# Clustered attention and two mixtures: tile sizes in one pool, and a new order of stack copies, centroids and dots

## The chip, the cores and the metric

The kernel runs on one core of a Trainium2 chip, as one program. The metric is device microseconds for one execution, from the first to the last instruction with what lies around it; smaller is better. The profiler names the engines PE (TensorE, matmuls and transposes), PEld (TensorE's weight loads), DVE (VectorE), ACT (ScalarE), POOL (GpSimd) and SP (SyncE, which issues nearly all DMAs here).

## The reference

Attention with B=2, H=8, S=768, D=64 comes first; each query and key is given to the nearest of 16 centroids of its head, and a query sees the keys of its own cluster only. The result, as 1536 rows of 512, goes through two layers of the form (g(x @ w_in)) @ w_out, with 2048 columns between.

```python
q_n, k_n, c_n = (a / (norm(a) + 1e-6) for a in (q, k, centroids))
q_assign = argmax(einsum('bhsd,hcd->bhsc', q_n, c_n), -1)      # k_assign alike
mask = q_assign[:, :, :, None] == k_assign[:, :, None, :]
scores = where(mask, q @ k.T / sqrt(D), -1e9)
attn = softmax(scores) @ v                                     # then [1536, 512]
h = x @ w1_in;  x = (h * cos(h)) @ w1_out
h = x @ w2_in;  g = where(h >= 1, h, where(h <= -1, 0, (h + 1)**2 / 4));  out = g @ w2_out
```

## The kernel before

**Order.** The program sets each engine's order itself: an engine runs its instructions as the Python code writes them (`manual_schedule`). What stands first in a queue and waits holds up all that is behind it; this goes for SP's queue of DMA issues too.

**Attention.** There are 8 pairs (batch, two heads) and 16 cycles d = 0 to 15; a cycle is one head of a pair, 12 row tiles of scores. A cycle's order is a string of words, run by `run_cycle`: `S` scores of a row tile (4 matmuls, then DVE's row maximum), `E` its exponential on ACT, `T` and `t` a transposed tile of probabilities (copied out of PSUM by ACT or by DVE), `V` the product with v, `R` the inverse row sums (DVE, then POOL writes `line`, then SP stores it to DRAM as `flat`), `B` SP reads `flat` back, spread over 64 partitions, as `rb`, `X` DVE multiplies V's result by `rb`, `Y` POOL splits that into `xh` and `xl`, `W` and `w` a step of the weights' conversion, `P` the next step of preparing a pair, `K` the copies for a pair's second head. Even cycles run EVEN, odd ones ODD; the first is BEGIN, the last three have strings of their own.

**A pair's preparation** (`prep_pair`) has 12 steps. Steps 1 to 4 transpose q and k (`ptq`, L492), copy them out as `t32` (L498) and split them on POOL into `th` (L474) and `tl` (L475). Steps 5 and 6 are the dots with the centroids: matmuls `dt` (L513), ACT's copy `dc` (L516), transposes `pd` (L520). Steps 7 to 11 find the nearest centroid on DVE and POOL (`eq`, L532, is POOL's; the maximum after it, L537, and `dots`, L539, are DVE's); step 9 also issues `stack_head(0)`, four copies by SP (L470) from `th` and `tl` into the stacked operands `st0` and `st1` of the first head. Step 12 transposes the result to `oht` and copies it into the stacks, `one_hots(0)`, four small copies. For the second head, `stack_head(1)` and `one_hots(1)` together are one entry of the list `second`, which `K` runs. `th` and `tl` are one buffer each; pairs 1, 3 and 5 use the memory of a weight tile instead, so only pair 7 must wait until the copies out of pair 6's `th` and `tl` are done.

**The first pair** (`first_pair`) is prepared ahead of the cycles. `centroid_setup` normalises the centroids by a chain of small DVE steps (L265 to L275) after ACT's square root (L260). After the root, ACT runs an Exp (L262) whose result nobody reads: it loads ACT's table, and it writes two elements of `nat1`, so that the load of the second pair's q and k, into the same tile, has to wait for it. Its input is `y`, the column that L265 then overwrites.

**The mixtures.** A unit is `hidden` (h = x w_in for 512 columns and 512 rows) or `output` (y = g w_out): 48 matmuls of 512 columns in 4 groups, three per product, since x, w and g are each a high and a low fp32r part. A layer has 12 units of each kind, and hidden and output take turns. `hidden` multiplies the weights with `xh` and `xl`; `output` multiplies them with `gh` and `gl`. Four weight tiles go round: slices qi = 0 and 2 use `w_0` (hidden) and `w_1` (output), qi = 1 and 3 use `w_2` and `w_3`.

**Memory.** Tiles lie in a partition one behind the other, by pools. Ahead of `xpool` stand `xh`, `xl`, `w_0`, `w_1` and the weights' loading tiles, all at multiples of 512 bytes. `xpool` holds, in bytes per partition, `rec` 128, `den` 3 x 128, `turned` 128, `line` 512 and `rb` 2 x 1536: 4224, which is 8 x 512 + 128. What is allocated behind it, attention's tiles and, after attention, the mixtures' (`w_2`, `w_3`, `gh`, `gl`, the sums and scratch), follows from there: the mixtures' tiles all start 128 bytes behind a multiple of 512.

Of the kernel before, what the change touches and what calls it, by code (L numbers as in the profile page):

```python
# [9 lines left out]
F32 = mybir.dt.float32  # L10
# [4 lines left out]
AF = mybir.ActivationFunctionType  # L15
# [4 lines left out]
P = 128  # L20
# [13 lines left out]
def attention_moe_moe(  # L34
# [19 lines left out]
    B, H, S, D = q.shape  # L54
# [22 lines left out]
    desc = cpool.tile([P, C], F32, name="desc")  # L77
# [56 lines left out]
    xpool = ctx.enter_context(tc.tile_pool(name="xpool", bufs=1))  # L134
# [70 lines left out]
    with ExitStack() as actx:  # L205
# [48 lines left out]
        def centroid_setup(ct):  # L254
            sq = ct[:, 1]
            nc.vector.tensor_tensor(sq, ct[:, 0], ct[:, 0], ALU.mult)
            ss = ap.tile([P, 32], F32, tag="css", name="css")
            nc.vector.tensor_reduce(ss[:, 0:1], sq, AX.X, ALU.add)
            y = ss[:, 1:2]
            sq = nc.scalar.activation(y, ss[:, 0:1], AF.Sqrt)  # L260
            nat[1] = [w0pool.tile([P, 2, NJ, 2, D], F32, tag="wraw", bufs=1, name="nat1")]
            nc.scalar.activation(nat[1][0][:, :, 0, 0, 0:1].rearrange("p s o -> p (s o)"),  # L262
                                 y.to_broadcast([P, 2]), AF.Exp, scale=0.0)
            for _ in range(2):
                nc.vector.tensor_scalar(y, y, 1e-30, None, ALU.max)  # L265
                nc.vector.reciprocal(ss[:, 2:3], y)
                nc.vector.scalar_tensor_tensor(
                    ss[:, 3:4], ss[:, 0:1], ss[:, 2:3], y, ALU.mult, ALU.add)
                nc.vector.tensor_scalar(y, ss[:, 3:4], 0.5, None, ALU.mult)
            nc.vector.tensor_scalar(ss[:, 2:3], y, 1e-6, None, ALU.add)  # L270
            nc.vector.reciprocal(ss[:, 3:4], ss[:, 2:3])
            cd = ap.tile([P, HS], F32, tag="pt", bufs=PT_BUFS, name="cd")[:, :P].rearrange(
                "p (r d) -> p r d", r=2)
            for r in range(2):
                done = nc.vector.tensor_scalar(cd[:, r], ct[:, 0], ss[:, 3:4], None, ALU.mult)  # L275
            return cd, done

        prepped = {}
        second = []

        def first_pair():
# [28 lines left out]
            def bank(name):  # L310
                return pool_q.tile([P, HS], F32, tag="q", name=name)
# [5 lines left out]
            def turn(s, hf):  # L317
                qk[s, hf] = bank(f"qk0_{s}_{hf}")
                for jj in range(HJ):
                    nc.tensor.transpose(qk[s, hf][:, jj * P:(jj + 1) * P],  # L320
                                        t[:, s, hf * HJ + jj].rearrange("p h d -> p (h d)"), ident)
# [7 lines left out]
            pc = ps_t.tile([P, HS], F32, tag="t", name="pc")[:, :P]  # L329
            turn(0, 0)  # L330
            turn(0, 1)
            nc.tensor.transpose(pc, cd.rearrange("p r d -> p (r d)"), ident)
            turn(1, 0)
            turn(1, 1)
            run_idle(NIDLE[1])
            pcv = pc.rearrange("p (g h c) -> p g h c", h=2, c=C)
# [3 lines left out]
            for s, hf in ((0, 0), (0, 1), (1, 0)):  # L340
                nc.scalar.activation(t32[s][hf], qk[s, hf], AF.Copy,
                                     scale=D ** -0.5 if s == 0 else 1.0)
# [109 lines left out]
        def prep_pair(i):  # L452
# [4 lines left out]
            if i in (1, 3, 5):  # L457
                t2 = w0pool.tile([P, 2, 2, S], F32R, tag="w_1", name=f"t2_{i}")
# [10 lines left out]
            def copy(dst, src):  # L469
                nc.sync.dma_start(dst.bitcast(F32), src.bitcast(F32))  # L470
# [6 lines left out]
            def stack_head(h):  # L477
                rows = slice(h * D, (h + 1) * D)
                t = st[h][0]
                copy(t[0:D], th[rows, 0].unsqueeze(1).to_broadcast([D, 2, S]))  # L480
                copy(t[D:P, 0], tl[rows, 0])
                t = st[h][1]
                copy(t[0:D, 0], th[rows, 1])
                copy(t[D:P, 0], th[rows, 1])
                copy(t[0:D, 1], tl[rows, 1])
# [65 lines left out]
            def one_hots(h):  # L551
                for s in range(2):
                    for par in range(2):
                        r0 = par * 64 + s * 32 + h * C
                        dst = st[h][s][D:D + C, 1].rearrange(
                            "c (par jp n) -> c par jp n", par=2, n=P)[:, par]
                        copy(dst, oht[r0:r0 + C])

            def second_head():
                stack_head(1)  # L560
                one_hots(1)

            one_hots(0)
            second.append(second_head)
            yield

        units = [(i, h, hf) for i in range(len(pairs)) for h in range(2) for hf in range(2)]
# [24 lines left out]
        def row_exp(n):  # L592
            s, nm = ptile[n]
            d, jj = divmod(n, NJ)
            if jj == 0:
                dens[d] = xpool.tile([P, 32], F32, tag="den", bufs=3, name=f"den{d}")
            p = ap.tile([P, 2, HS], F32, tag="p", bufs=P_BUFS, name=f"p{n}")
            nc.scalar.activation(p, s[:, :, :HS], AF.Exp, bias=nm,  # L598
                                 accum_out=dens[d][:, jj:jj + 1])
            ptile[n] = p  # L600
# [23 lines left out]
        dens = {}  # L624
# [47 lines left out]


        NDBL = len(units) // 2
        rec = xpool.tile([P, 32], F32, tag="rec", name="rec")
        nc.gpsimd.memset(rec, 0.0)
        made = chain.from_iterable(prep_pair(i) for i in range(1, len(pairs)))

# [2 lines left out]
        def scores_of(n):  # L681
            scores(n, 0)
            scores(n, 1)
            row_max(n)

        def run_cycle(d, order):


            for word in order.split():
                what, arg = word[0], int(word[1:] or 0)  # L690
                n = NJ * d + arg
                if what == "S":
                    if n < NJ * NDBL:
                        scores_of(n)
                elif what == "E":
                    if n < NJ * NDBL:
                        row_exp(n)
                elif what in "Tt":
                    p_transpose(2 * d + arg // NJ, arg % NJ, what == "t")
                    next_slot()  # L700
                elif what == "P":
                    next(made, None)
                elif what == "R":
                    inverse(d)
                elif what == "V":
                    p_v(d)
                elif what == "X":
                    if opsum:
                        x_rows(min(opsum))
                elif what == "K":  # L710
                    if second:
                        second.pop(0)()
                elif what == "B":
                    spread()
                elif what == "Y":
                    if x32s:
                        x_parts()
                elif what in "Ww":
                    pump(1 if d >= FIRST + (what == "w") else 0)
                elif what == "N":  # L720
                    next_slot()
            if d == 3:
                issue_chunk(0)

        PRE = "P S8 P E8"
        BEGIN = "S3 P T0 T1 S4 E3 P T2 E4 P T3 S5 E5 t4 T5 S6 T6 T7 E6 P R S7 t8 T9 E7 T10 P S8 P E8 B P S9 P t11 S10 V E9 E10"
        EVEN = "P S5 T0 T1 P t2 E5 S6 T3 P T4 E6 t5 S7 R T6 P T7 E7 S8 X T8 T9 E8 Y t10 B S9 P w P E9 t11 S10 W E10 V"
        ODD = "K S5 T0 T1 P t2 S6 E5 T3 X T4 t5 S7 Y E6 P T6 R E7 T7 S8 P E8 t8 T9 S9 T10 B P t11 E9 W S10 V P P E10 W"
        LATE_ODD = "S5 T0 T1 t2 E5 S6 T3 K R T4 t5 S7 X Y E6 T6 T7 E7 S8 E8 t8 T9 S9 T10 B t11 S10 E9 V W W W E10"
        LATE_EVEN = "S5 T0 t1 t2 E5 S6 T3 T4 E6 R T5 S7 X Y E7 T6 S8 T7 t8 W S9 E8 t9 B T10 E9 t11 W S10 V E10 W"  # L730
        LAST = "S5 T0 E5 t1 T2 T3 X t4 R t5 Y t6 T7 t8 B T9 t10 T11 W V W W W X Y"
        first_pair()
        for d in range(-1, NDBL):
            run_cycle(d, PRE if d < 0 else BEGIN if d == 0 else
                      {13: LATE_ODD, 14: LATE_EVEN, 15: LAST}.get(d, (EVEN, ODD)[d % 2]))
        manual.close()
# [138 lines left out]
```

## Time and profile before

| | |
|---|---|
| time, median of 3 runs | 785.4 us (784.46 to 785.62) |
| the profiled execution's own time | 787.31 us |
| its span, first to last instruction | 785.5 us |
| PE busy | 770.9 us, 98% |
| DVE, ACT, POOL busy | 569.5, 361.3, 254.9 us |
| mean granted TensorE clock | 0.993 |

PE's 98% is an average over two unlike parts: attention until about 262 us, in which PE has short gaps, and the mixtures, in which it has none. A granted clock of 1.00 is 2.4 GHz, 0.50 is 1.2 GHz. In the rows below an arrow reads "out<-in"; in brackets stands how long the engine was idle before the instruction and what released it.

### The profile page before, as it was taken

The numbers are of one execution on the slowest core, as the hardware profiler recorded it, in microseconds if no ns is written. First come the engines' busy times: TensorE is split into PE (matmuls) and PEld (weight loads), VectorE is DVE, ScalarE is ACT, GpSimd is POOL, SyncE is SP. The second block draws the span as 40 slices with busy tenths as digits, with TensorE's granted clock in tenths as the row PEclk, the third lists the DMA queues.
The fourth block names the chain that finished last, engine by engine and source line by source line (L and its number), as shares of the span: only waits on it lengthen the run. The fifth ranks groups of instructions, "written<-read, shape, count | busy, mean of one in ns | idle before, by whom it ended". The sixth has DMA issues, their size and how long they took to land.

```text
span 785.5 us, 10592 instructions
## 1 busy us (share of the span) xinstructions
PE 770.9 (98%) x3885; PEld 609.9 (78%) x3886; DVE 569.5 (73%) x824; ACT 361.3 (46%) x671; POOL 254.9 (32%) x390
## 2 busy tenths in 40 slices
PE   8899999999899999999999999999999999999998
PEld 4677777776676888888888888888888888888886
DVE  5767688797688778687788887888867787555552
ACT  4867677777574644534334342333434232212220
POOL 5447449465534522222222123422312121111110
PEclk9999999999899999999999999999999999999999
DMA  8874676665342122213131122021121111000012
GB/s 193 215 160 120 181 156 183 155 174 123 86 130 75 54 108 75 86 55 108 53 101 62 54 78 83 3 104 55 54 101 61 53 54 55 0 1 1 27 41 93
DMA packets 49523, 70.10 MB, mean 89 GB/s; under 512 B 28576, under 2 KB 33664, under 8 KB 49472
## 3 DMA queue, kind: packets, MB, share of 16 engines
q1 hardware_dynamic: 49328, 69.40, 31.5%
q8 instruction: 30, 0.49, 0.3%
q14 instruction: 21, 0.17, 0.1%
q10 hardware_dynamic: 144, 0.03, 0.0%
HBM read 46.17 MB, written 3.19 MB: 63 GB/s over the span
## 4 chain that ended last, share of the span: by engine, by line
PE 89%; ACT 4%; DVE 3%; DMA 2%; issue 1%; SPq 0%; POOL 0%; ACTq 0%; DVEq 0%
PE h L785 11%; PE h L787 11%; PE y L787 11%; PE h L786 11%; PE y L786 11%; PE y L785 11%; PE o L649 7%; PE pt L635 5%; PE s L580 4%; PE s L583 3%; ACT p L598 2%; ACT p_t L640 1%; DVE nm L589 1%; PE ptq L492 1%; DMA wraw<-in_moe_w_in_dram 1%
## 5 line engine op out<-in xcount | busy, mean ns | idle before, releaser
L747 POOL TENSOR_SCALAR gh<-g 128x512 fp32r<-128x512 f32 x96 | 71.4, 744 | 294.5 <-DVE g L778 161.0
L785 PE MATMUL h<-xh,w 128*128 128x512 f32 x384 | 150.6, 392 | 0.2 <-ACT p L598 0.2
L787 PE MATMUL h<-xh,w 128*128 128x512 f32 x384 | 150.7, 393 | 0.0
L786 PE MATMUL h<-xl,w 128*128 128x512 f32 x384 | 150.6, 392 | 0.0
L589 DVE TENSOR_REDUCE nm<-s 128x1 f32<-128x768 f32 x96 | 91.3, 952 | 45.4 <-PE s L583 43.7
L598 ACT ACTIVATE p<-s,nm 128x768 f32<-128x768 f32 x96 | 87.2, 909 | 23.6 <-DVE nm L589 20.2
L774 ACT ACTIVATE p<-h,ones 128x512 f32<-128x512 f32 x48 | 33.1, 690 | 136.7 <-DVE m L773 136.3
L751 DVE TENSOR_TENSOR gl<-g,gh 128x512 fp32r<-128x512 f32 x96 | 72.1, 751 | 21.5 <-POOL gh L747 16.0
L635 PE MATMUL pt<-ident,p 128*128 128x128 f32 x576 | 82.2, 278 | 3.4 <-DVE p_t L638 2.9
L787 PEld LDWEIGHTS h<-xh,w 128*128 128x128 f32 x384 | 72.1, 188 | 16.6 <-issue 0.6
L785 PEld LDWEIGHTS h<-xh,w 128*128 128x128 f32 x384 | 72.1, 188 | 16.4 <-issue 0.4
L786 PEld LDWEIGHTS h<-xl,w 128*128 128x128 f32 x384 | 72.2, 188 | 16.1
L635 PEld LDWEIGHTS pt<-ident,p 128*128 128x128 f32 x576 | 68.6, 143 | 12.1 <-ACT p L598 4.0
L640 ACT ACTIVATE p_t<-pt 128x384 f32<-128x384 f32 x126 | 57.8, 491 | 43.2 <-PE pt L635 42.3
L580 PE MATMUL s<-st,st 128*128 128x384 f32 x192 | 74.6, 388 | 1.6 <-ACT p L598 1.0
L787 PE MATMUL y<-gh,w 128*128 128x512 f32 x192 | 75.3, 392 | 0.0
L786 PE MATMUL y<-gl,w 128*128 128x512 f32 x192 | 75.3, 392 | 0.0
L785 PE MATMUL y<-gh,w 128*128 128x512 f32 x192 | 75.3, 392 | 0.0
L785 PE MATMUL y<-w,gh 128*128 128x512 f32 x192 | 75.3, 392 | 0.0
L787 PE MATMUL y<-w,gl 128*128 128x512 f32 x192 | 75.2, 392 | 0.0
L786 PE MATMUL y<-w,gh 128*128 128x512 f32 x192 | 75.2, 392 | 0.0
L824 DVE TENSOR_TENSOR acc<-y,acc 128x512 f32<-128x512 f32 x72 | 49.2, 685 | 35.6 <-PE y L787 35.6
(120 smaller groups left out, 1310.7 us busy)
## 6 DMA issues: line engine op xcount, KB each, us to landing
wraw<-in_moe_w_in_dram SPq DMA_DIRECT2D x16, 1024.0 KB
wraw<-in_moe_w_out_dram SPq DMA_DIRECT2D x16, 1024.0 KB, 4.7
st<-t SPq DMA_DIRECT2D x24, 192.0 KB, 4.3
st<-th SPq DMA_DIRECT2D x10, 384.0 KB, 3.8
st<-th SPq DMA_DIRECT2D x20, 192.0 KB, 3.9
st<-tl SPq DMA_DIRECT2D x19, 192.0 KB
nat<-in_q_dram SPq DMA_DIRECT2D x8, 384.0 KB, 4.1
nat<-in_k_dram SPq DMA_DIRECT2D x8, 384.0 KB, 4.8
```

Of the source, the lines that this page charges most:

```text
L580: nc.tensor.matmul(s[:, step, :HS], qt[:, 0, cols], kt[:, 0, kc], start=True, stop=False)
L589: nc.vector.tensor_reduce(nm, s[:, :, :HS], AX.XY, ALU.max, negate=True)
L598: nc.scalar.activation(p, s[:, :, :HS], AF.Exp, bias=nm, accum_out=dens[d][:, jj:jj + 1])
L635: nc.tensor.transpose(ps[:, jj * P:(jj + 1) * P], p[:, kt * P:(kt + 1) * P], ident)
L640: nc.scalar.activation(pt, ps, AF.Copy)
L649: nc.tensor.matmul(o[hf * D:(hf + 1) * D], prepped[i][0][:, h, kt], pts.pop((2 * d + hf, kt)), start=kt == 0, stop=kt == NJ - 1)
L747: nc.gpsimd.tensor_scalar(hi, g, 1.0, 0.0, ALU.mult, ALU.add)
L751: nc.vector.tensor_tensor(lo, g, hi.bitcast(F32), ALU.subtract)
L785: nc.tensor.matmul(o, lh, rh, start=first, stop=False)
L786: nc.tensor.matmul(o, lh, rl, start=False, stop=False)
L787: nc.tensor.matmul(o, ll, rh, start=False, stop=last)
L824: nc.vector.tensor_tensor(a, po, a, ALU.add)
```

## The change

1. `rec` gets 64 columns, of which the first 32 are used (256 bytes); `den` gets 8 columns and four buffers (4 x 32 bytes). `xpool` is then 256 + 128 + 128 + 512 + 3072 = 4096 bytes, and every tile behind it starts 128 bytes earlier: the mixtures' tiles at multiples of 512, attention's p, st, th and v at 128 behind one instead of 256.
2. L262's Exp reads `desc` instead of `y`.
3. In `first_pair` the transposes of k's first half, `turn(1, 0)`, stand ahead of the centroids' transpose `pc`.
4. The second pair's steps 5 and 6 run behind the first and second scores instead of in and behind PRE.
5. `stack_head(1)` and `one_hots(1)` are separate entries of `second`, pushed at steps 9 and 12; the `K`s stand in the even cycle (after E7 and after B) instead of at the start of the odd one. In BEGIN, `B` comes ahead of S8.
6. In ODD, `X` moves from behind T3 to behind T7 and `Y` from behind S7 to behind S8. In LATE_EVEN the last `W` stands ahead of `V`.

```diff
-                                 y.to_broadcast([P, 2]), AF.Exp, scale=0.0)
+                                 desc[:, 0:2], AF.Exp, scale=0.0)
...
+            turn(1, 0)
             nc.tensor.transpose(pc, cd.rearrange("p r d -> p (r d)"), ident)
-            turn(1, 0)
...
             scores_of(0)
+            next(made)
             scores_of(1)
+            next(made)
...
             stack_head(0)
+            second.append(stack_head)
...
-            def second_head():
-                stack_head(1)
-                one_hots(1)
-
             one_hots(0)
-            second.append(second_head)
+            second.append(one_hots)
...
-                dens[d] = xpool.tile([P, 32], F32, tag="den", bufs=3, name=f"den{d}")
+                dens[d] = xpool.tile([P, 8], F32, tag="den", bufs=4, name=f"den{d}")
...
-        rec = xpool.tile([P, 32], F32, tag="rec", name="rec")
+        rec = xpool.tile([P, 64], F32, tag="rec", name="rec")[:, :32]
...
-                        second.pop(0)()
+                        second.pop(0)(1)
...
-        PRE = "P S8 P E8"
-        BEGIN = "... t8 T9 E7 T10 P S8 P E8 B P S9 P t11 S10 V E9 E10"
-        EVEN = "P S5 T0 T1 P t2 E5 S6 T3 P T4 E6 t5 S7 R T6 P T7 E7 S8 X T8 T9 E8 Y t10 B S9 P w P E9 t11 S10 W E10 V"
-        ODD = "K S5 T0 T1 P t2 S6 E5 T3 X T4 t5 S7 Y E6 P T6 R E7 T7 S8 P E8 t8 T9 S9 T10 B P t11 E9 W S10 V P P E10 W"
-        LATE_ODD = "S5 T0 T1 t2 E5 S6 T3 K R T4 ..."
+        PRE = "S8 E8"
+        BEGIN = "... t8 T9 E7 T10 P B S8 P E8 P K S9 K P t11 S10 V E9 E10"
+        EVEN = "P S5 T0 T1 P t2 E5 S6 T3 P T4 E6 t5 S7 R T6 P T7 E7 K S8 X T8 T9 E8 Y t10 B K S9 P w P E9 t11 S10 W E10 V"
+        ODD = "S5 T0 T1 P t2 S6 E5 T3 T4 t5 S7 E6 P T6 R E7 T7 X S8 Y P E8 t8 T9 S9 T10 B P t11 E9 W S10 V P P E10 W"
+        LATE_ODD = "S5 T0 T1 t2 E5 S6 T3 R T4 ..."
```

How this moves instructions, at three places. PE in the first pair, before and after; `qk` are the transposes of q (0) and k (1), `idle` is filler.

```order
19 L320 MATMUL qk0_0_0_182<-ident_60,nat0_99 128x128 x3
20 L320 MATMUL qk0_0_1_186<-ident_60,nat0_99 128x128 x3
21 L332 MATMUL pc_181<-ident_60,cd_159 128x128
22 L320 MATMUL qk0_1_0_191<-ident_60,nat0_99 128x128 x3
23 L320 MATMUL qk0_1_1_195<-ident_60,nat0_99 128x128 x3
```

```order
19 L320 MATMUL qk0_0_0_182<-ident_60,nat0_99 128x128 x3
20 L320 MATMUL qk0_0_1_186<-ident_60,nat0_99 128x128 x3
21 L320 MATMUL qk0_1_0_190<-ident_60,nat0_99 128x128 x3
22 L333 MATMUL pc_181<-ident_60,cd_159 128x128
23 L320 MATMUL qk0_1_1_195<-ident_60,nat0_99 128x128 x3
```

`pc` has three transposes of k ahead of it instead of behind it.

SP's queue of issues in cycle 10, before and after; `rb10` is the inverse sums of cycle 10, `st0_6_1` and `st1_6_1` the stacks of pair 6's second head.

```order
112 L614 DMA flat10_2514<-line10_2509 6x128
113 L241 DMA v32_7_2522<-in_v_dram 128x2x384
114 L470 DMA st0_6_0_2174<-oht6_2528 16x384 x2
115 L470 DMA st1_6_0_2175<-oht6_2528 16x384 x2
116 L622 DMA rb10_2575<-flat10_2514 64x384 x2
117 L470 DMA st0_6_1_2176<-th6_2172 64x2x768
118 L470 DMA st0_6_1_2176<-tl6_2173 64x768
119 L470 DMA st1_6_1_2177<-th6_2172 64x768 x2
120 L470 DMA st1_6_1_2177<-tl6_2173 64x768
```

```order
112 L613 DMA flat10_2514<-line10_2509 6x128
113 L241 DMA v32_7_2522<-in_v_dram 128x2x384
114 L472 DMA st0_6_0_2183<-oht6_2528 16x384 x2
115 L472 DMA st1_6_0_2184<-oht6_2528 16x384 x2
116 L472 DMA st0_6_1_2185<-th6_2181 64x2x768
117 L472 DMA st0_6_1_2185<-tl6_2182 64x768
118 L472 DMA st1_6_1_2186<-th6_2181 64x768 x2
119 L472 DMA st1_6_1_2186<-tl6_2182 64x768
120 L621 DMA rb10_2580<-flat10_2514 64x384 x2
```

The stack copies and `rb10` have changed places.

POOL in cycle 11, before and after; `th7` and `tl7` are pair 7's parts, `xh`, `xl` and `rb10` the five instructions of `Y`, `eq7` is step 8 of pair 7.

```order
154 L668 TENSOR_SCALAR xh_73<-rb10_2575 64x384
155 L669 TENSOR_TENSOR xl_74<-rb10_2575,xh_73 64x384
156 L664 TENSOR_SCALAR rb10_2575<-rb10_2575 64x384
157 L668 TENSOR_SCALAR xh_73<-rb10_2575 64x384
158 L669 TENSOR_TENSOR xl_74<-rb10_2575,xh_73 64x384
159 L474 TENSOR_SCALAR th7_2585<-t32_7_1_1_2729 128x384
160 L475 TENSOR_TENSOR tl7_2586<-t32_7_1_1_2729,th7_2585 128x384
161 L611 TENSOR_SCALAR line11_2743<-turned11_2741 6x32 x4
162 L532 TENSOR_TENSOR eq7_2837<-eq7_2837,desc_61 128x384
```

```order
154 L476 TENSOR_SCALAR th7_2594<-t32_7_1_1_2723 128x384
155 L477 TENSOR_TENSOR tl7_2595<-t32_7_1_1_2723,th7_2594 128x384
156 L610 TENSOR_SCALAR line11_2737<-turned11_2735 6x32 x4
157 L667 TENSOR_SCALAR xh_73<-rb10_2580 64x384
158 L668 TENSOR_TENSOR xl_74<-rb10_2580,xh_73 64x384
159 L663 TENSOR_SCALAR rb10_2580<-rb10_2580 64x384
160 L667 TENSOR_SCALAR xh_73<-rb10_2580 64x384
161 L668 TENSOR_TENSOR xl_74<-rb10_2580,xh_73 64x384
162 L534 TENSOR_TENSOR eq7_2837<-eq7_2837,desc_61 128x384
```

The five instructions of `Y` now stand behind pair 7's last parts and `line11`; `eq7` is the last of them in both.

## Rows read from the trace of the kernel before

**Rows 1.** The page's first part: busy time and instructions of each engine.

```profile
PE 770.9 (98%) x3885; PEld 609.9 (78%) x3886; DVE 569.5 (73%) x824; ACT 361.3 (46%) x671; POOL 254.9 (32%) x390
```

**Rows 2.** Timeline of PE, first matmuls of units: start us, us, engine, line, out<-in.

```profile
295.69 0.40 PE L785 MATMUL y<-gh,w 128*128 128x512 f32 x1
...
306.88 0.40 PE L785 MATMUL h<-xh,w 128*128 128x512 f32 x1
...
318.07 0.40 PE L785 MATMUL y<-gh,w 128*128 128x512 f32 x1
...
340.47 0.39 PE L785 MATMUL y<-gh,w 128*128 128x512 f32 x1
...
351.36 0.40 PE L785 MATMUL h<-xh,w 128*128 128x512 f32 x1
...
538.64 0.40 PE L785 MATMUL y<-w,gh 128*128 128x512 f32 x1
...
549.80 0.39 PE L785 MATMUL h<-xh,w 128*128 128x512 f32 x1
...
560.69 0.40 PE L785 MATMUL y<-w,gh 128*128 128x512 f32 x1
```

**Rows 3.** Start of the program: timelines of ACT, DVE, PE, SP; one DMA row.

```profile
2.94 0.20 ACT L260 ACTIVATE css<-css 128x1 f32<-128x1 f32 x1 [0.51 <-DVE css L258]
...
4.69 0.15 DVE L265 TENSOR_SCALAR css<-css 128x1 f32<-128x1 f32 x1 [1.78 <-ACT nat L262]
...
7.61 0.36 PE L332 MATMUL pc<-ident,cd 128*128 128x128 f32 x1 [1.38 <-DVE cd L275]
...
1.55 0.83 SPq L225 DMA_DIRECT2D nat<-in_k_dram  x1
...
nat<-in_k_dram SPq DMA_DIRECT2D x8, 384.0 KB, 4.8
```

**Rows 4.** Windows: stretch, its us, busy PE, PEld, DVE, ACT, POOL, PEclk, DMA share, GB/s.

```profile
4.40:7.70 3.30, 1.39 (x9) 0.73 (x8) 2.52 (x12) 1.12 (x4) 1.19 (x3) 1.00 1.08 219
7.80:11.10 3.30, 3.30 (x14) 1.68 (x17) 2.02 (x5) 1.36 (x3) 1.67 (x3) 0.50 0.95 233
20.00:23.00 3.00, 1.26 (x10) 0.90 (x7) 2.38 (x4) 2.94 (x8) 2.65 (x4) 1.00 0.94 278
199.00:202.30 3.30, 0.97 (x8) 0.69 (x6) 0.47 (x1) 1.61 (x4) 2.53 (x6) 1.00 0.00 1
202.40:209.10 6.70, 6.20 (x25) 6.01 (x26) 4.46 (x9) 3.67 (x8) 0.83 (x4) 0.50 0.76 172
```

**Rows 5.** Timelines of SP and PE around cycle 0's last scores.

```profile
34.24 2.48 SPq L470 DMA_DIRECT2D st<-oht  x4
...
42.53 0.34 PE L583 MATMUL s<-st,st 80*128 80x384 f32 x1
```

**Rows 6.** Cycles 10 to 12: timelines of SP, POOL and PE.

```profile
180.70 1.12 SPq L622 DMA_DIRECT2D rb<-flat  x2
...
185.42 0.88 SPq L470 DMA_DIRECT2D st<-tl  x1
...
188.75 0.51 POOL L474 TENSOR_SCALAR th<-t 128x384 fp32r<-128x384 f32 x1 [7.98 <-DMA st<-th]
...
200.81 0.99 POOL L532 TENSOR_TENSOR eq<-eq,desc 128x384 f32<-128x384 f32 x1
...
202.90 0.90 PE L635 MATMUL pt<-ident,p 128*128 128x128 f32 x3 [2.93 <-DVE p_t L638]
```

**Rows 7.** Inverse sums in cycles 4, 5 and 11: DVE, SP, and the DMA row.

```profile
188.51 0.21 DVE L608 STREAM_TRANSPOSE turned<-rec 128x32 f32<-128x32 f32 x1
...
75.00 0.21 DVE L608 STREAM_TRANSPOSE turned<-rec 128x32 f32<-128x32 f32 x1
...
62.68 2.47 SPq L470 DMA_DIRECT2D st<-oht  x4
...
rb<-flat SPq DMA_DIRECT2D x32, 96.0 KB, 2.7
```

More of the change, by code (lines that the diff above doesn't have):

```diff
@@ L723, in run_cycle @@
                 issue_chunk(0)
-        PRE = "P S8 P E8"
-        BEGIN = "S3 P T0 T1 S4 E3 P T2 E4 P T3 S5 E5 t4 T5 S6 T6 T7 E6 P R S7 t8 T9 E7 T10 P S8 P E8 B P S9 P t11 S10 V E9 E10"
-        EVEN = "P S5 T0 T1 P t2 E5 S6 T3 P T4 E6 t5 S7 R T6 P T7 E7 S8 X T8 T9 E8 Y t10 B S9 P w P E9 t11 S10 W E10 V"
-        ODD = "K S5 T0 T1 P t2 S6 E5 T3 X T4 t5 S7 Y E6 P T6 R E7 T7 S8 P E8 t8 T9 S9 T10 B P t11 E9 W S10 V P P E10 W"
-        LATE_ODD = "S5 T0 T1 t2 E5 S6 T3 K R T4 t5 S7 X Y E6 T6 T7 E7 S8 E8 t8 T9 S9 T10 B t11 S10 E9 V W W W E10"
-        LATE_EVEN = "S5 T0 t1 t2 E5 S6 T3 T4 E6 R T5 S7 X Y E7 T6 S8 T7 t8 W S9 E8 t9 B T10 E9 t11 W S10 V E10 W"
+        PRE = "S8 E8"
+        BEGIN = "S3 P T0 T1 S4 E3 P T2 E4 P T3 S5 E5 t4 T5 S6 T6 T7 E6 P R S7 t8 T9 E7 T10 P B S8 P E8 P K S9 K P t11 S10 V E9 E10"
+        EVEN = "P S5 T0 T1 P t2 E5 S6 T3 P T4 E6 t5 S7 R T6 P T7 E7 K S8 X T8 T9 E8 Y t10 B K S9 P w P E9 t11 S10 W E10 V"
+        ODD = "S5 T0 T1 P t2 S6 E5 T3 T4 t5 S7 E6 P T6 R E7 T7 X S8 Y P E8 t8 T9 S9 T10 B P t11 E9 W S10 V P P E10 W"
+        LATE_ODD = "S5 T0 T1 t2 E5 S6 T3 R T4 t5 S7 X Y E6 T6 T7 E7 S8 E8 t8 T9 S9 T10 B t11 S10 E9 V W W W E10"
+        LATE_EVEN = "S5 T0 t1 t2 E5 S6 T3 T4 E6 R T5 S7 X Y E7 T6 S8 T7 t8 W S9 E8 t9 B T10 E9 t11 W S10 W V E10"
         LAST = "S5 T0 E5 t1 T2 T3 X t4 R t5 Y t6 T7 t8 B T9 t10 T11 W V W W W X Y"
```

## The prediction

> **What bounds the kernel now.** I read the page's first part first [rows 1]: PE is busy 98% of the span. So time can only come from two places: PE's matmuls themselves get quicker, or one of PE's few gaps closes. Next came the windows of PE by stage [rows 4] and the timeline of PE in the mixtures [rows 2]. From about 262 us on PE has no gap at all; there the question is how long a unit of 48 matmuls takes. Before that, in attention, three stretches stand out: the start (PE busy 1.39 of 3.30 us, then a stretch at clock 0.50), the stretch at 20 to 23 us (1.26 of 3.00), and the hole at 200 us (0.97 of 3.30, then 6.70 us at clock 0.50). For each I followed back what ended PE's wait [rows 3, 6]. The sum is made against the median of the runs shown, 785.4 us. The profiled execution took 787.31 us with a span of 785.5, so a span stands some 2 us below its own run; I take differences of the span over to the median as they are.
>
> **Part 1, the offsets: 6.8 us less.** The kernel before holds a comparison of its own. Units follow each other without a gap, so the distance from one start to the next is a unit's time [rows 2]. With w_1 (at a multiple of 512) against gh (128 behind one): 295.69 to 306.88, 11.19 us. With w_2 (128) against xh (0): 306.88 to 318.07, again 11.19. With w_3 and gh, both 128 behind one: 340.47 to 351.36, 10.89. In the second layer, gh against w_1: 538.64 to 549.80, 11.16; w_0 against xh, both at 0: 549.80 to 560.69, 10.89. So a unit is slow where the two operands stand at different offsets and fast where they stand at the same, 0 or 128; the kind of unit doesn't matter, since hidden and output are found on both sides. Half of the 24 units of a layer are of the unlike sort (output at qi = 0 and 2, hidden at qi = 1 and 3, three blocks each). After the change all of these tiles are at 0. That is 12 x (11.19 - 10.89) = 3.6 us in the first layer and 12 x (11.16 - 10.89) = 3.2 in the second. All of it lies on the path, as PE has no gap there. What could be late next is a weight tile or DVE's part of g; the fast units run at 10.89 with the same work beside them, so I subtract nothing. Bounds: nothing (see the third rival) to 7.2, 0.30 for each of 24. In attention the tiles behind xpool all move by the same 128 bytes, so p and st against each other stay as they are; against ident, which stays, they change, which I put at 0, between -1 and +1.
>
> **Parts 2 and 3, the start: 2.2 us less.** ACT's root ends at 2.94 + 0.20 = 3.14; DVE's L265 starts at 4.69, after 1.78 us idle, and the releaser is the Exp of L262, which reads what L265 overwrites [rows 3]. With desc as its input, L265 can start near 3.2, and the centroids are ready 1.5 earlier: 6.1 where pc started at 7.61. But pc now stands behind three transposes of k, whose load was issued at 1.55 and lands 4.8 later by its median, near 6.35. I take pc at 7.0, 0.6 earlier, with three transposes already done. The larger share is the clock: PE's stretch from 7.80 to 11.10 is busy throughout at 0.50, half speed [rows 4], and what came before it is a stretch of 1.39 in 3.30, with a gap of 1.38 for pc. The gap shrinks to some 0.3, with the transposes of k in it. If the clock then stays at 1.00, up to 3.30 / 2 = 1.65 comes back. 0.6 + 1.6 = 2.2. Bounds: 0.6 with the clock lost all the same, 3.2 if pc needs no wait for k and dots and copies follow at once.
>
> Does it reach the end of attention? What follows at the start is bound by ACT and the DMAs (ACT busy 2.94 of 3.00 and a DMA share of 0.94 at 20 to 23 us) [rows 4]. The second pair's earlier dots (part 4) take pd out of that window; since ACT is full there I give them nothing, between 0 and 0.7 less. The last meeting place is the second pair's one-hots: SP ends their issue at 34.24 + 2.48 = 36.72, and PE needs them at 42.53 [rows 5]. There BEGIN's new order puts rb0, two issues and a wait for flat, ahead of them. An issue of rb takes 1.12 [rows 6]; with the wait I put 2.4 on the one-hots, so they stay where they are while PE comes 2.2 earlier. The 5.8 us between shrink to 3.6, still some more than a copy's landing needs by rb's 2.7 [rows 7]. So the gain survives, narrowly.
>
> **Part 5, the stack copies: 1.2 less, 0.3 back, and the clock, 2.6.** The hole at 200 us starts far ahead of it. POOL's L474 of pair 7 waits 7.98 us, until 188.75, for the copies out of pair 6's th and tl; from there POOL is busy without a pause to eq, 200.81 + 0.99 = 201.80; DVE's maximum waits for eq, p_t's copy stands behind it on DVE, and PE, idle for 2.93, starts at 202.90 [rows 6]. After the change stack_head(1) goes into rb10's place at 180.70, so it starts by rb10's 1.12 earlier, and POOL's chain with it. The chain holds the same instructions in another order with eq last, so it ends 1.2 earlier: PE starts at 201.7, the hole is 1.75. In exchange rb10 goes behind the copies. They took from 181.82 to 185.42 + 0.88 = 186.30, 4.5 us; rb10 is issued at 185.2 to 186.3 and lands 2.7 later, near 189.0 [rows 6, 7]. X, moved behind R in DVE's order, comes up at 188.51 + 0.21 = 188.72 [rows 7]. DVE waits 0.3, and behind it the row maximum of S8, which PE's next scores need: 0.3 lost, bounds 0 to 1. In the other odd cycles the room is larger: cycle 4's one-hots end at 62.68 + 2.47 = 65.15, so rb4 lands near 65.2 + 4.5 + 1.1 + 2.7 = 73.5, against X at 75.2 [rows 7], 1.7 us to spare. That is why X and Y can go so late. K in the even cycle's SP queue holds up flat and the weights' loads by some us; both have that room.
>
> The clock after the hole: 6.70 us at 0.50 with PE busy 6.20 [rows 4]. At full speed that is up to 3.1 less; DVE has 4.46 us of work in it, so at least 2.2 comes back. I take 2.6. Whether it comes back hangs on the hole of 1.75. Rows stand on both sides: the start (3.30 - 1.39 = 1.91 us idle) was followed by 0.50, as was the hole (3.30 - 0.97 = 2.33 idle), while the stretch from 20 to 23 us (3.00 - 1.26 = 1.74 idle) kept 1.00. A hole of 1.75 is nearest to the last. I hold that likelier than not, two to one.
>
> Part 6 beside X and Y: W ahead of V changes no order on DVE or ACT that PE sees; 0.
>
> **The sum**: 785.4 - 6.8 - 2.2 - 1.2 + 0.3 - 2.6 = 772.9 us.
>
> **Rivals.**
> First, the clock falls in the hole all the same: 772.9 + 2.6 = 775.5. For it speaks that the stretch at the start fell with as much PE work as the one at 20 us that held.
> Second, the start and part 5 bring only their waits' lengths: SP is the bound there (DMA share 0.94 to 1.08 [rows 4]), the one-hots behind rb0 take the 2.2 back, and the clock falls: 785.4 - 6.8 - 1.2 + 0.3 = 777.7. Against it stands the 3.6 us left for the landing.
> Third, the offsets do nothing, and what I read as their effect is something else that alternates with qi: 772.9 + 6.8 = 779.7. PE would then read its two operands at a rate that doesn't depend on where they lie. Against it: the same code at the same line is fast and slow by the tile alone, in both layers, in both kinds of unit [rows 2]. The Trainium skill, in "SBUF — State Buffer", section "SBUF: two separate sides", says of PE that it never waits on anyone at the engine ports, and its port table gives the moving operand and the weight load independent read ports; by that, where operands lie would not matter and this rival would hold. The rows of 11.19 and 10.89 speak against taking it that far.
> Fourth, slower than before: with the stack copies ahead of rb in every even cycle, X waits on DVE in each of the 7 odd cycles, and the row maxima behind it stop PE, whose scores have two buffers. It decides from a loss of 2.0 us a cycle: 7 x 2.0 = 14.0 cancels the gain (786.9); rb would have to land some 4 us later than in my count (1.7 of room, 2.0, and some slack). At 2.5 us a cycle the time is 772.9 + 17.5 = 790.4. Against it: copies issue within 4.5 us where rows show them.
>
> **How the numbers follow.** Forecast (clock holds) 0.54, its own range 770.2 to 774.9 from the bounds of the start (0.6 to 3.2), of X's wait (0 to 1) and of attention's offsets (1 either way); first rival 0.28; second 0.08; third 0.07; fourth 0.03. The range 769.5 to 778.5 holds the forecast, the first and the second rival with their bounds, and leaves out the last two. A measurement of this kernel can tell about 0.2%, 1.6 us, from no change: every case but the fourth is faster by more, save 0.03 of the third's 0.07, in which the gains in attention fail as well and nothing is left. So faster 0.94, same 0.03, slower 0.03.
>
> **What would show it.** Every unit of the mixtures at 10.9 us, layer two too, is part 1; some units at 11.2 would refute it, and this is what makes the prediction most wrong. L265 near 3.2, pc near 7.0 waiting for k's transposes, and 7.8 to 11 us at clock 1.00: the start. PE's second one-hot matmul near 40.3 without a wait: the start's gain is kept. L474 of pair 7 at 187.6 less what the start has won, a hole of 1.75 and the granted clock behind it: part 5 and the first rival. DVE idle ahead of X in odd cycles, released by the DMA of rb: the fourth.

## The result, and the profile after

The changed kernel takes 773.85 us, median of four executions (772.78 to 778.12), against 785.35 of the kernel before (four, 784.46 to 785.62): ratio 0.9866, 95% interval 0.9827 to 0.9904. The forecast was 772.9, with a range of 769.5 to 778.5. In a second comparison, beside its own parts, it took 773.51 (773.04 to 775.16) against 786.38: ratio 0.9837, interval 0.9806 to 0.9869. The slowest execution, 778.12, had a mean granted clock of 0.995; the other seven had 0.998 to 1.000.

The profiled execution of after took 773.20 us with a span of 771.4; that of before 787.31 with 785.5. First comes the page of after, which answers to [rows 1]: PE has 10.6 us less work and is busy 99% of the span; the other engines' work is what it was.

```profile
PE 760.3 (99%) x3885; PEld 606.6 (79%) x3886; DVE 570.0 (74%) x824; ACT 360.0 (47%) x671; POOL 254.6 (33%) x390
```

Where the span's 14.1 us went is read from PE's timeline, at the first matmul of `V` in cycles 0, 11 and 12 (before, then after):

```profile
36.05 0.54 PE L649 MATMUL o<-p_t,v 128*64 128x384 f32 x2
...
192.61 0.54 PE L649 MATMUL o<-p_t,v 128*64 128x384 f32 x2
...
211.85 0.54 PE L649 MATMUL o<-p_t,v 128*64 128x384 f32 x2
```

```profile
33.26 0.54 PE L648 MATMUL o<-p_t,v 128*64 128x384 f32 x2
...
190.54 0.55 PE L648 MATMUL o<-p_t,v 128*64 128x384 f32 x2
...
205.10 0.54 PE L648 MATMUL o<-p_t,v 128*64 128x384 f32 x2
```

| stretch | before | after | difference |
|---|---|---|---|
| start to V of cycle 0 | 36.05 | 33.26 | -2.79 |
| to V of cycle 11 | 156.56 | 157.28 | +0.72 |
| to V of cycle 12 (the hole) | 19.24 | 14.56 | -4.68 |
| to the first hidden matmul (245.18, 238.52) | 33.33 | 33.42 | +0.09 |
| from there to the end (785.5, 771.4) | 540.3 | 532.9 | -7.4 |

**The mixtures.** The starts of units in after, PE's timeline, answer to [rows 2]: three in the first layer, three in the second. From the first output of `after` to the last every unit takes 10.88 us; those that took 11.15 to 11.20 are gone.

```profile
266.95 0.39 PE L784 MATMUL y<-gh,w 128*128 128x512 f32 x1
...
277.83 0.39 PE L784 MATMUL h<-xh,w 128*128 128x512 f32 x1
...
288.71 0.39 PE L784 MATMUL y<-gh,w 128*128 128x512 f32 x1
...
538.95 0.39 PE L784 MATMUL h<-xh,w 128*128 128x512 f32 x1
...
549.83 0.39 PE L784 MATMUL y<-w,gh 128*128 128x512 f32 x1
...
560.71 0.39 PE L784 MATMUL h<-xh,w 128*128 128x512 f32 x1
```

**The start**, DVE, PE and two windows of after, against [rows 3, 4] (columns of the windows as there). L265 waits for the root alone, pc stands behind nine transposes without a wait, and the granted clock is 1.00 in both stretches.

```profile
3.26 0.15 DVE L265 TENSOR_SCALAR css<-css 128x1 f32<-128x1 f32 x1 [0.27 <-ACT css L260]
...
5.00 1.70 PE L320 MATMUL qk<-ident,nat 128*128 128x128 f32 x9
6.54 0.27 PE L333 MATMUL pc<-ident,cd 128*128 128x128 f32 x1
```

```profile
4.40:7.70 3.30, 3.19 (x18) 1.95 (x16) 1.87 (x10) 2.07 (x6) 1.36 (x3) 1.00 0.91 208
...
7.80:11.10 3.30, 3.26 (x24) 1.85 (x25) 2.06 (x6) 1.65 (x4) 2.24 (x3) 1.00 1.10 269
```

**The hole**, SP, POOL, DVE and PE of after around cycles 10 to 12, against [rows 6, 7]. The copies of pair 6's second head start at 176.99, right behind the one-hots; POOL starts pair 7's parts at 184.01 and ends eq at 197.30; PE is idle for 0.51 instead of 2.93, and the clock stays at 1.00. X follows L607 on DVE without a wait. First two rows of SP before, then those of after.

```profile
176.79 3.58 SPq L470 DMA_DIRECT2D st<-oht  x4
...
181.87 0.67 SPq L470 DMA_DIRECT2D st<-th  x1
```

```profile
174.35 2.54 SPq L472 DMA_DIRECT2D st<-oht  x4
176.99 0.67 SPq L472 DMA_DIRECT2D st<-th  x1
...
184.01 0.51 POOL L476 TENSOR_SCALAR th<-t 128x384 fp32r<-128x384 f32 x1 [5.38 <-ACT p L597]
...
196.29 1.01 POOL L534 TENSOR_TENSOR eq<-eq,desc 128x384 f32<-128x384 f32 x1
...
186.31 0.21 DVE L607 STREAM_TRANSPOSE turned<-rec 128x32 f32<-128x32 f32 x1
186.44 0.53 DVE L653 TENSOR_TENSOR rb<-o,rb 128x384 f32<-128x384 f32 x1
...
198.41 0.55 PE L634 MATMUL pt<-ident,p 128*128 128x128 f32 x3 [0.51 <-DVE p_t L637]
```

```profile
198.70:205.40 6.70, 6.26 (x42) 5.21 (x42) 6.44 (x12) 5.61 (x12) 2.99 (x7) 1.00 0.46 100
```

**The clock moves from execution to execution.** Each execution comes with its mean granted clock. Of thirty executions of the kernel before, beside the experiments, those at a mean of 0.999 took 783.4 to 783.8 us, those at 0.996 785.6 to 786.4, at 0.993 787.0 to 788.5, and at 0.990 and 0.989 789.0 to 790.8; a straight line through all thirty gives 0.65 us for each 0.001. At half speed for t us the mean is 1 - 0.5 t / 785, so 0.999, 0.996 and 0.993 are 1.6, 6.3 and 11 us of half speed. The profiled execution of before, at 0.993, is one in which the clock fell both at the start and behind the hole. In the profiled execution of after, at 0.999, the clock falls only behind PE's last matmul (0.72 from 769.0 us to the end), where it costs nothing. Below, "at equal clock" means the distance from that line, averaged over a kernel's executions; since the means are given to 0.001, a difference of half a microsecond in it says little.

### The profile page after: what moved, and what is told of

Read it like the earlier page. It is cut to its first block, busy times and chain, and to the rows that moved or that the text cites. A ratio compares the mean times of both kernels' runs of the same rounds, so it can differ in the third digit from the quotient of the medians.

```text
span 771.4 us, 10598 instructions
## 1 busy us (share of the span) xinstructions
PE 760.3 (99%) x3885; PEld 606.6 (79%) x3886; DVE 570.0 (74%) x824; ACT 360.0 (47%) x671; POOL 254.6 (33%) x390
## 4 chain that ended last, share of the span: by engine, by line
PE 79%; DMA 6%; SPq 3%; POOL 3%; DVE 3%; ACT 3%; issue 1%; ACTq 0%; POOLq 0%; DVEq 0%
PE h L784 11%; PE h L786 11%; PE h L785 11%; PE y L785 11%; PE y L784 11%; PE y L786 11%; PE o L648 4%; PE pt L634 2%; SPq L472 2%; PE s L579 2%; DMA flat<-line 2%; ACT p L597 2%; PE s L582 2%; DMA st<-tl 1%; DMA st<-t 1%
## 5 line engine op out<-in xcount | busy, mean ns | idle before, releaser
L750 DVE TENSOR_TENSOR gl<-g,gh 128x512 fp32r<-128x512 f32 x96 | 73.7, 768 | 22.3 <-POOL gh L746 16.3
L154 ACT ACTIVATE wx<-wraw 128x1024 f32<-128x1024 f32 x32 | 36.5, 1141 | 84.3 <-DVE w L173 33.8
```

The costliest lines, as they stand in the source:

```text
L154: nc.scalar.activation(x, high.bitcast(F32), AF.Abs)
L750: nc.vector.tensor_tensor(lo, g, hi.bitcast(F32), ALU.subtract)
```

## The experiments

### The parts alone, and the whole on the same chip

`offsets` is the kernel before with the new sizes alone; `start` the kernel before with the Exp's input and the order of `pc`; `order` the changed kernel with the sizes and the start of the kernel before.

```diff
# offsets
-                dens[d] = xpool.tile([P, 32], F32, tag="den", bufs=3, name=f"den{d}")
+                dens[d] = xpool.tile([P, 8], F32, tag="den", bufs=4, name=f"den{d}")
...
-        rec = xpool.tile([P, 32], F32, tag="rec", name="rec")
+        rec = xpool.tile([P, 64], F32, tag="rec", name="rec")[:, :32]
# start
-                                 y.to_broadcast([P, 2]), AF.Exp, scale=0.0)
+                                 desc[:, 0:2], AF.Exp, scale=0.0)
...
+            turn(1, 0)
             nc.tensor.transpose(pc, cd.rearrange("p r d -> p (r d)"), ident)
-            turn(1, 0)
```

> The kernel before with the sizes of rec and den alone. If like offsets of a matmul's two operands are what makes a unit quick, every unit of the mixtures takes 10.88 to 10.89 us and the time is 785.4 - 7.4 = 778.0 us, with the hole at 200 us and the clock behind it as before. If the offsets do nothing and the quicker units of the changed kernel come from its order, units still alternate between 10.89 and 11.19 and the time stays at 785.4.

> The kernel before with the Exp that reads desc and the transposes of k ahead of pc, nothing else. My theory: pc near 6.5 us, the granted clock at 1.00 from 7.8 us on, the first V 2 us earlier or more, and this lasts to the end of attention: 783.2 us. Rival: the start is taken back by the one-hots' copies of the second pair or at the hole of 200 us (a DMA's or POOL's time that does not move), and the time is 785.0 to 785.4.

> The changed kernel with the offsets and the start as before: only the order of stack copies, rb, X, Y and the second pair's dots. My theory: the hole at 200 us shrinks from 2.9 to 0.5 or so, the granted clock stays at 1.00 behind it, and V of cycle 12 stands 4.7 us earlier relative to V of cycle 11: 780.7 us. Rival: the hole shrinks only because the start moved SP's queue into a better phase; then it is 1.2 to 2 us here, and the time 783 to 784.5.

> The changed kernel itself, beside its parts on one chip. If the parts add up, its gain over the kernel before is the sum of theirs, 7.4 + 2.2 + 4.7 = 14.3 us by the profiled executions (771.1), within 1 us; if they lean on each other (the hole closes only with the start), the parts alone sum to less than the whole by 2 us or more.

| kernel | median us | range | ratio to before (786.38), interval | at equal clock |
|---|---|---|---|---|
| offsets | 780.98 | 779.62 to 784.24 | 0.9928 (0.9902 to 0.9954) | -5.9 |
| start | 786.03 | 784.05 to 787.22 | 0.9995 (0.9980 to 1.0010) | -0.2 |
| order | 781.71 | 781.0 to 782.9 | 0.9938 (0.9916 to 0.9959) | -2.3 |
| again (the whole) | 773.51 | 773.04 to 775.16 | 0.9837 (0.9806 to 0.9869) | -10.0 |

The parts' medians sum to -5.4 - 0.35 - 4.7 = -10.4, the whole has -12.9. That the parts lean on each other is not shown by this: each of the four intervals reaches 1 to 2.6 us to either side. At equal clock the sum is -8.4 against -10.0, and most of that difference is that `offsets` stays 1.5 behind what its units gain, -7.4.

**offsets**: all units take 10.88 us, with the order of the kernel before; so it is the sizes that make them quick. In `start` and `order`, with the old sizes, slow and quick units still alternate. Its median is 2 us less good than the units say. In its profiled execution, the slowest of its six, attention is 4.1 us longer than before (first hidden matmul at 249.29 instead of 245.18): pc waited 3.29 us for the centroids and the hole was 3.65, each followed by a granted clock of 0.50.

```profile
9.01 0.47 PE L332 MATMUL pc<-ident,cd 128*128 128x128 f32 x1 [3.29 <-DVE cd L275]
...
207.44 0.90 PE L635 MATMUL pt<-ident,p 128*128 128x128 f32 x3 [3.65 <-DVE p_t L638]
...
277.71 0.39 PE L785 MATMUL y<-gh,w 128*128 128x512 f32 x1
...
288.59 0.39 PE L785 MATMUL h<-xh,w 128*128 128x512 f32 x1
```

**start**: the theory fell. Here is where its gain went, PE's and POOL's timeline and a window of that run:

```profile
20.69 0.59 PE L520 MATMUL pd<-ident,dc 128*128 128x128 f32 x2 [1.43 <-ACT dc L516]
...
188.65 0.52 POOL L474 TENSOR_SCALAR th<-t 128x384 fp32r<-128x384 f32 x1 [8.96 <-ACT p_t L640]
...
203.04 0.90 PE L635 MATMUL pt<-ident,p 128*128 128x128 f32 x3 [4.16 <-DVE p_t L638]
```

```profile
20.90:24.90 4.00, 4.00 (x19) 3.87 (x18) 1.98 (x3) 1.91 (x5) 0.00 (x0) 0.58 1.11 269
```

The clock stayed at 1.00 up to 20.9 us, and then fell behind the wait for the second pair's dots. V of cycle 0 still stood 0.97 earlier than before, and V of cycle 11 1.08. But POOL's L474 starts at 188.65, where it stood at 188.75 [rows 6]: PE comes earlier to a hole whose end has not moved, waits 4.16 instead of 2.93, and V of cycle 12 is left 0.21 earlier. The rival named the place rightly: the hole.

**order**: the hole is 0.53 with the old start too, and the clock is 1.00 behind it. That speaks against the rival: the new order closes the hole by itself. Its start had the centroids' wait as before (0.74 for pc in this execution), and the clock did not fall there. Sizes aside, `order` and the changed kernel differ by the start alone, and their holes are alike: here the start's gain is kept, 0.80 at V of cycle 0 (34.06 against 33.26) and 0.87 at V of cycle 12 (205.97 against 205.10); in `again` it is 0.44 and 0.85.

```profile
199.28 0.55 PE L634 MATMUL pt<-ident,p 128*128 128x128 f32 x3 [0.53 <-DVE p_t L637]
```

### What of the offsets counts

`equal` moves all tiles of the mixtures by 128 bytes; `mixed` gives three distances in one kernel; `atoffs` leaves the mixtures at multiples of 512 and puts attention's tiles back to where they were.

```diff
# equal
+    pad = cpool.tile([P, 32], F32, name="pad")
     xh = cpool.tile([P, NPAIR, NT], F32R, name="xh")
# mixed
-    wslot += [mp.tile([P, 2, 4, 512], F32R, name=f"w_{n}") for n in range(2, 4)]
+    for n, pad in ((2, 16), (3, 56)):
+        mp.tile([P, pad], F32, name=f"pad{n}")
+        wslot.append(mp.tile([P, 2, 4, 512], F32R, name=f"w_{n}"))
+    mp.tile([P, 64], F32, name="pad4")
# atoffs
+        ap.tile([P, 32], F32, name="pad")
         ps_s = []
```

> The changed kernel with 128 bytes put ahead of xh, so that every tile of the mixtures starts 128 bytes behind a multiple of 512. If it is the likeness of the two operands' offsets that counts, all units stay at 10.88 us and the span at 771 to 772. If it is the multiple of 512 itself, every unit becomes slow, 11.16 to 11.19, and the span grows by 45 x 0.3 = 13 us.

> The changed kernel with pads among the mixtures' tiles: w_2 at 64 bytes behind a multiple of 512, w_3 at 288, gh and gl at 32, the rest at 0. So hidden is at distance 0 for even qi and 64 for odd qi, output at 32 for even qi and 256 for odd qi. If any unlike offset costs what 128 did, only hidden at even qi stays at 10.88 us and the rest take 11.16 to 11.19. If the cost follows the distance, output at even qi (32) is between, hidden at odd qi (64) higher, and output at odd qi (256) the highest or, if 256 is a period, at 10.88.

> The changed kernel with 128 bytes put ahead of attention's tiles, so that these stand where they did in the kernel before (probabilities at 256 behind a multiple of 512, their transposes at 128) and the mixtures' at multiples of 512. The sizes alone brought 5.4 us by the medians, where the units of the mixtures brought 7.4. If attention's own offsets take the difference, this kernel is 1.5 to 2 us quicker than the changed one: 771.5 to 772. If the difference is only the clock's falls in other executions, it stays at 773.5, within 0.5.

`equal` (one execution, 774.83 us): all units at 10.88. The multiple of 512 is not needed; likeness is. PE's timeline:

```profile
268.55 0.39 PE L785 MATMUL y<-gh,w 128*128 128x512 f32 x1
...
279.43 0.39 PE L785 MATMUL h<-xh,w 128*128 128x512 f32 x1
```

`mixed` (one execution, 781.75 us), PE's timeline from output (0, 0) on:

```profile
266.96 0.40 PE L787 MATMUL y<-gh,w 128*128 128x512 f32 x1
...
278.17 0.40 PE L787 MATMUL h<-xh,w 128*128 128x512 f32 x1
...
289.08 0.40 PE L787 MATMUL y<-gh,w 128*128 128x512 f32 x1
...
300.29 0.39 PE L787 MATMUL h<-xh,w 128*128 128x512 f32 x1
...
311.48 0.40 PE L787 MATMUL y<-gh,w 128*128 128x512 f32 x1
...
333.87 0.40 PE L787 MATMUL y<-gh,w 128*128 128x512 f32 x1
...
344.80 0.39 PE L787 MATMUL h<-xh,w 128*128 128x512 f32 x1
```

Distance 32 (266.96 to 278.17): 11.21 us. Distance 0 (278.17 to 289.08): 10.91. Distance 64 (300.29 to 311.48): 11.19. Distance 256 (333.87 to 344.80): 10.93. So 32 and 64 bytes cost as much as 128 does, and 256 next to nothing: neither of the two expectations whole, but 256 is a period or near it, as the second allowed. Whether 0.02 is left at 256 can't be told: over the whole run units at 256 took 10.91 to 10.93, those at distance 0 10.89 to 10.92.

`atoffs` (773.79 us, 772.9 to 774.35, against 773.51 of the changed kernel; the kernel before had medians of 786.95 and 786.38 beside them): attention's own offsets change nothing that can be measured. The 1.5 us by which `offsets` stays behind its units (-5.9 against -7.4) is therefore not theirs. Longer waits in some of its executions would do it, but its one trace can't show that; it stays open.

### The Exp and the dots

`noexp` is the changed kernel with the Exp reading y again; `nodots` the changed kernel with the second pair's steps 5 and 6 in and behind PRE.

```diff
# noexp
-                                 desc[:, 0:2], AF.Exp, scale=0.0)
+                                 y.to_broadcast([P, 2]), AF.Exp, scale=0.0)
# nodots
             scores_of(0)
-            next(made)
             scores_of(1)
-            next(made)
...
-        PRE = "S8 E8"
+        PRE = "P S8 P E8"
```

> The changed kernel with the Exp reading y again, so that the centroids wait for it as before. My theory: pc comes 1 us later, near 7.6, and with the earlier dots of the second pair most of that stays: 774.5 to 775.5 us, more if the granted clock falls at the start. Rival: the start is covered by SP and POOL further on, and the time stays at 773.5.

> The changed kernel with the second pair's steps 5 and 6 where they were, in and behind PRE. In the run with the start alone the granted clock fell at 20.9 us, behind a gap of 1.4 us in which the transposes of those dots waited for ACT. My theory: the earlier dots keep the start's gain; without them PE waits 1.4 us near 19 us, the clock falls there in some executions, and the time is 774.5 to 776. Rival: ACT is the bound there, and the time stays at 773.5.

`noexp` took 773.89 us (772.99 to 774.84). L265 waits for the Exp as in the kernel before, and pc comes 0.45 to 0.7 later (7.24 against 6.54 and 6.79 in two executions of the changed kernel), but PE waits only 0.16 for it, since k's transposes now stand ahead. The Exp's input alone brings nothing that can be measured; the order of pc covers the wait.

```profile
4.71 0.15 DVE L265 TENSOR_SCALAR css<-css 128x1 f32<-128x1 f32 x1 [1.79 <-ACT nat L262]
...
7.24 0.33 PE L333 MATMUL pc<-ident,cd 128*128 128x128 f32 x1 [0.16 <-DVE cd L275]
```

`nodots` took 774.38 us (774.22 to 775.85). PE waits 1.43 for ACT near 20 us, as in the kernel before, yet the clock stayed at 1.00 there in the profiled execution. The median is 0.9 above the changed kernel's, which the two ranges don't quite part: the earlier dots are worth a microsecond at most, and the clock's fall at 20.9 us in `start` was not a matter of this wait alone. Nor do the earlier dots and the new start rule such a fall out: in the profiled execution of `equal`, which has both, the clock was 0.50 from about 23 to 26 us, behind waits of 1.05 and 0.52 us for ACT, and V of cycle 0 stood at 35.71 instead of 33.26 (a wait of 1.24 us for a copy, at 15.7 us, had its part in that).

```profile
20.46 0.33 PE L520 MATMUL pd<-ident,dc 128*128 128x128 f32 x1 [1.43 <-ACT dc L516]
```

A window of `equal`:

```profile
24.00:25.00 1.00, 1.00 (x5) 0.90 (x4) 0.18 (x1) 1.00 (x3) 0.68 (x1) 0.50 1.34 230
```

### The hole, its size and the clock

`hole1` and `hole2` put one or two more POOL instructions into pair 7's chain; `rbfirst` gives cycle 10 the old order of SP's issues.

```diff
# hole1 (range 1), hole2 (range 2)
+            for _ in range(1 if i == len(pairs) - 1 else 0):
+                nc.gpsimd.tensor_tensor(eq, eq, eq, ALU.mult)
             nc.gpsimd.tensor_tensor(
                 eq, eq, desc.unsqueeze(1).to_broadcast([P, G, C]), ALU.mult)
# rbfirst, for d == 10 alone
         EVEN = "... P T7 E7 K S8 X T8 T9 E8 Y t10 B K S9 ..."
+        EVEN_RB = "... P T7 E7 S8 X T8 T9 E8 Y t10 B K K S9 ..."
```

> The changed kernel with one more POOL instruction (eq times eq, 128x384, which leaves eq as it is) ahead of pair 7's eq, so that the hole at 197 us widens by 1.0 to 1.1 us, from 0.51 to 1.6: near the hole that the prediction forecast. If the prediction's two to one is right, the granted clock stays at 1.00 behind it and the time grows by the hole alone, 773.5 + 1.1 = 774.6. If such a hole lowers the clock, 2 to 2.6 us come on top: 777.

> The changed kernel with two such POOL instructions: a hole of 2.6 to 2.7 us, nearly that of the kernel before (2.93). If the clock's fall hangs on the hole, it falls here to 0.50 for some 6.7 us in most executions: 773.5 + 2.1 + 2.3 = 778. If it hangs on something else of the kernel before, the clock stays and the time is 775.6.

> The changed kernel with cycle 10's copies in the old order: rb10 ahead of pair 6's second head, all else as changed. The prediction's account: the copies and POOL's chain start 1.1 to 1.9 us later, the hole at 197 us grows from 0.51 to 1.7 or 2.4, and the time is 774.7 to 775.4 with the clock at 1.00, 777 with a fall. Rival: SP's place in the queue was not what closed the hole, but the copies landing sooner after a quicker weight load; then the hole stays under 1 us and the time at 773.5.

| kernel | PE's hole in the profiled execution | us, median | mean clock of its executions |
|---|---|---|---|
| changed kernel | 0.51; 0.55 in `again` | 773.51 | 0.999 four times; in the first comparison 0.999, 0.995, 0.998, 1.000 |
| hole1 | 1.47 | 774.45 | 0.999, 0.999, 1.000, 0.997 |
| hole2 | 2.39 | 775.71 | 0.999, 0.998, 0.998, 0.996 |
| rbfirst | 3.07 | 775.51 | 0.998, 0.998, 0.998, 0.999 |

Beside these three the kernel before had a median of 786.38, as beside the changed kernel. Here are PE's timeline and a window behind the hole, `hole2` first; then `rbfirst`, with SP's and POOL's timeline, the window and a row of SP's waits between 170 and 190 us (what it waited for, us in total, times, longest):

```profile
200.09 0.55 PE L636 MATMUL pt<-ident,p 128*128 128x128 f32 x3 [2.39 <-DVE p_t L639]
```

```profile
199.90:206.00 6.10, 5.46 (x37) 4.75 (x37) 5.85 (x12) 4.84 (x11) 1.98 (x6) 1.00 0.25 56
```

```profile
173.64 2.57 SPq L472 DMA_DIRECT2D st<-oht  x4
177.77 1.13 SPq L621 DMA_DIRECT2D rb<-flat  x2
178.94 0.67 SPq L472 DMA_DIRECT2D st<-th  x1
...
186.09 0.51 POOL L476 TENSOR_SCALAR th<-t 128x384 fp32r<-128x384 f32 x1 [8.17 <-DMA st<-th]
...
200.25 0.33 PE L634 MATMUL pt<-ident,p 128*128 128x128 f32 x1 [3.07 <-DVE p_t L637]
```

```profile
200.80:205.50 4.70, 4.70 (x25) 4.54 (x25) 3.54 (x9) 3.79 (x8) 0.83 (x4) 0.64 0.62 134
```

```profile
SPq L621 <- DMA flat<-line: 1.2, 1, 1.2
```

A hole of 1.47 kept the clock, and the median is 0.9 higher, about the wait itself (the hole grew by 0.96, though the two kernels' ranges overlap). One of 2.39 kept it in the profiled execution (1.00 over 6.10 us behind it), and the median is 2.2 higher; one of its executions had a mean of 0.996, and where its clock fell is not recorded. In `rbfirst`, with 3.07, the clock fell to 0.50 for a stretch within 201 to 205 us (0.64 on the mean of the window). So behind the two longer holes the profiled clock went either way, and the executions of one kernel differ; that the fall hangs on the hole is likely, what decides it is not shown.

`rbfirst` also prices rb's place. The one-hots' issue ends at 173.64 + 2.57 = 176.21; rb10 goes out at 177.77, the copies at 178.94. In the changed kernel the copies follow the one-hots by 0.10 (174.35 + 2.54 = 176.89 to 176.99). So rb ahead of them costs 2.6 us here: 1.56 of waiting, which the trace puts mostly on the landing of `flat` in DRAM (1.2 us), and 1.17 of issue. The hole grows by 2.56 with it, more than either figure that was expected; the median grows by 2.0.

## Why the prediction came out right, point by point

- **Part 1, 6.8 less: the mechanism was right, the size a little low.** The stretch from the first hidden matmul on is 7.4 shorter; `offsets`, `equal` and `mixed` show that the distance of the two operands is the cause. The third rival, offsets do nothing, falls: 10.88 us against 11.15 to 11.21 for the same 48 matmuls. The sentence of the Trainium skill ("SBUF — State Buffer", section "SBUF: two separate sides") that PE never waits on anyone can't be taken to mean that it reads at one rate from wherever its operands lie. Attention's offsets, put at 0 between -1 and +1, show as nothing (`atoffs`).
- **Parts 2 and 3, 2.2 less: right in the profiles (-2.79 to the first V), wrong as something that the edit brings by itself.** Alone it brings 0.35, within its interval of nothing. The 1.6 for the clock was the error: with either start the clock falls in some executions and holds in others, as `order` (old start, 1.00) and `equal` (new start, 0.50 near 24 us) show. What the edit gains is kept where the hole is closed (0.87 between `order` and the changed kernel at V of cycle 12) and not where it is open (0.21 in `start`): the step "So the gain survives" looked at the one-hots of cycle 0, not at the hole, whose end is set by DMA copies and POOL and had not moved in `start`. At the one-hots the room was smaller than forecast too: in after their issue ends at 36.12 + 2.46 = 38.58 and PE's matmul stands at 40.04, 1.46 us instead of 3.6. It stands 0.56 behind the matmul ahead of it, against 0.26 before, so 0.3 was lost there.
- **Part 5, 1.2 less: too small by half.** The hole shrank by 2.42. In the kernel before, 1.50 us lie between the end of the one-hots' issue (176.79 + 3.58 = 180.37) and the copies (181.87), in the changed one 0.10: 1.40, where the prediction counted rb10's issue and not its wait. The other 1.04 is the one-hots' own issue, 2.54 instead of 3.58, which no term held; what it waited for is not shown. `rbfirst`, where the one-hots took 2.57 and rb waited 1.56, shows that rb's place alone is worth as much as both together. X's wait of 0.3 did not come.
- **The clock behind the hole, 2.6 less: 2.26 in the profiles** (4.68 - 2.42). Two to one that it holds was a fair guess. A hole of the forecast's 1.75 never came; the nearest, 1.47 in `hole1` and 2.39 in `hole2`, kept the clock in their profiled executions, as did the 0.5 of after, `again` and `order`. The first rival was therefore not the case in the profiles; in the execution of 778.12 us, at a mean of 0.995, the clock did fall somewhere, and where is not recorded.
- **Between V of cycle 0 and V of cycle 11** after took 0.72 more, 157.28 against 156.56. That is no cost of the new order that is shown: runs with it took from 156.44 (`equal`, `rbfirst`) to 157.55 (`atoffs`), runs with the old order from 156.45 (`start`) to 157.10 (`offsets`).
- **Profile against median.** The prediction took the profile's differences over to a median that stood 1.9 below the profiled execution (787.31 against 785.4). The profiled one had 11 us at half speed; the median's have less. The profiles differ by 14.1, the medians by 11.5, in the second comparison by 12.9. The terms that were too small and this one that was too large nearly cancelled: 12.5 was forecast. That the number was met is thus partly luck.
- **The forecast's own range** was given as 770.2 to 774.9; its bounds add up to 772.9 - 1.0 - 0.3 - 1.0 = 770.6 and 772.9 + 1.6 + 0.7 + 1.0 = 776.2. The measured time lies in either.
- The second and the fourth rival did not come: the gains at the start were not taken back in the changed kernel, and no odd cycle's X held up the row maxima; DVE waited 0.3 us once for rb in the whole execution.

## What to carry to other kernels

Where PE is busy without a gap, compare the time of like groups of matmuls by the tiles they use: a difference of 3% that follows the tile and not the code can be where tiles lie, and padding one small buffer may take it out. A gain ahead of a later wait whose end does not move becomes a longer wait there; look for what ends the next hole before counting on it. And before a stretch at half clock is counted as a gain, ask in how many executions it happens: take the mean granted clock of each, not of the profiled one.

## What the runs showed of the hardware that was not expected

- Matmuls of 512 columns in fp32r whose moving and stationary tiles lie at distances of 32, 64 or 128 bytes modulo 512 took 11.15 to 11.21 us for 48, at distance 0 10.88 to 10.92, at 256 10.91 to 10.93. What in the memory makes this is not shown.
- In `rbfirst` SP's issue of rb waited 1.56 us, 1.2 of it by the trace for a store to land in DRAM, and all issues behind it waited too; with rb's own issue of 1.17 this made PE's hole, some 20 us later, 3.07 instead of 0.51 us.
- The granted clock fell to 0.50 behind PE's holes of 2.93, 3.07, 3.65 and 4.16 us, and held at 1.00 behind holes of 0.51, 1.47 and 2.39 in the profiled executions. Behind waits near 1.4 us it did either: it fell at 20.9 us in `start` and not in `nodots`.
